# Attention and MLP on one core: token pairs side by side in the transposed tiles, the product with v in four pieces, and two moves in the MLP

## The chip, the core and the metric

The kernel runs on one core of one Trainium2 chip. The core has five engines that work side by side, each through its own list of instructions in order: TensorE (PE, with its weight loads shown apart as PEld), VectorE (DVE), ScalarE (ACT), GpSimd (POOL) and SyncE (SP), which here only issues DMAs. PE writes to the PSUM memory alone; DVE and ACT read from there; all else lies in SBUF. The metric is the device time of one execution in microseconds, lower being better.

## The reference

Eight batches of eight heads, 576 tokens, 64 elements a head. Nyström attention with 32 landmarks, then a layer norm and an MLP of 512 to 2048 to 512 with a residual:

```python
q_lm = q.reshape(B, H, m, S // m, D).mean(axis=3)      # m = 32, 18 tokens each
k_lm = k.reshape(B, H, m, S // m, D).mean(axis=3)
A  = sm(q, k_lm)            # softmax(scale * q @ k_lm^T)
Bm = sm(q_lm, k_lm)
C  = sm(q_lm, k)
Z = Bm.transpose(0, 1, 3, 2) / (norm_1(Bm) * norm_inf(Bm) + 1e-06)
for _ in range(6):
    Z = 2 * Z - Z @ Bm @ Z
x = A @ Z @ C @ v           # then heads side by side: [8, 576, 512]
xn = (x - mean) / sqrt(var + 1e-06) * g_ln
out = x + maximum(xn @ w_ch1, 0.0) @ w_ch2
```

## The kernel before

Two lines of work are woven together. The attention runs over five sets of batches, (0), (1), (2,3), (4,5), (6,7), as generators that `yield` a weight after each step. The MLP runs as one stream (`mlp`) over nine groups of 512 tokens; it yields after about every matmul. After an attention step of weight n, the main loop (L814 to L818) lets the stream take n times `rates[set]` steps. So PE's order is fixed by hand, and all matmuls are pinned in it (`MM`, `TR`: L67 and L71 in every profile). In the beginning the other engines are pinned too (`pin`, L63); from set (1) on (L794) the tile framework orders DVE, ACT and POOL itself.

A unit w is four heads of a batch. For sets (2,3) onward, `prep` (L457) makes the operands of the next set while this one runs: for k and for q of each unit, a DVE transpose in 32x32 blocks of 32-bit words (L465, two fp16 elements x of a head's 64 travel together) writes `xT`, and a DVE reduce (L469) sums the 18 tokens of each landmark into `lmk` or `lmq`. There are 8 such steps a set, 24 in all; `plans` says at which attention steps they, and the loads of q, k and v of the coming batches, are released (L806 to L810).

`attention2` (L494) then computes, in steps: the landmark softmax (`psb`); the scores of the landmarks with all keys, two units a step (`scores`, tiles `psec`), whose exponentials ACT writes to `ec` (L490) and DVE transposes into `ecT` (L528); the norm of the landmark matrix (`psse`); the product with v (`pscv`, L553 to L565), 288 matmuls of 32x32 weights on 65 columns, without a yield inside; six steps of the iteration (`psn`, with DVE's `st`, L587), the first two of which also make the scores of the queries (`psea`, `ea`); the combined matrix (`zcbd`, L605); and, in `rows_of` (L431), ten steps that give rows x of 128 tokens (`psy`, `xblk`), with the layer norm's statistics (`block_done`).

In the transposed tile, position (j, l, x) holds token 18l + j, so a fixed j gives 32 tokens that are 18 apart. ACT writes the exponentials in the order (b, l, x) with j = 2b + x, from scores that lie as (j, l).

In the MLP, POOL makes the normalised rows `xn` (for group 0, ACT does), PE transposes them into `psxt`, and DVE copies that to `xnT` (L680). Then `psh` = w1 x `xnT` in 64 matmuls on 512 columns, ACT's Relu into `hT` (L726), `pso` = `hT` x w2 in four blocks of 16 matmuls, and DVE adds the residual into `ot` (L744). Group 0 works on 128 columns at a time, since its blocks come one after the other. `psh`, `psxt` and `pso` share three PSUM buffers.

Of the kernel before, what the change touches and what calls it, by code (L numbers as in the profile page):

```python
# [20 lines left out]
def kernel(  # L21
# [58 lines left out]
    def act(*args, **kw):  # L80
        pin(nc.scalar.activation(*args, **kw))  # L81
# [375 lines left out]
    def prep(bs):  # L457
        units = [(b, u) for b in bs for u in range(U)]
        lm = {nm: asm.tile([P, len(units), LM, 2], FP16, name="lm" + nm, tag="lm" + nm)
              for nm in ("q", "k")}  # L460
        xT = {}
        for w, (b, u) in enumerate(units):
            for nm in ("k", "q"):
                t = aprep.tile([P, SEG, LM, 2], FP16, name="xT", tag="xT")
                nc.vector.transpose(  # L465
                    t[:].rearrange("p j l x -> p (j l x)").bitcast(UINT32),
                    nat_tiles[b][nm, u][:].rearrange("p j d -> p (j d)").bitcast(UINT32))
                with nc.allow_low_precision("landmark sums are rounded once, to fp16"):
                    nc.vector.tensor_reduce(out=lm[nm][:, w, :, :].rearrange("p l x -> p (l x)"),  # L469
                                            in_=t[:].rearrange("p j l x -> p (l x) j"),  # L470
                                            axis=AX.X, op=ALU.add)
                xT[nm, w] = t
                yield lm, xT

    def scores(pair, lm, xT, sc, name):
        tiles = {w: ps2.tile([P, SEG, LM], FP32, name="ps" + name, tag="p2") for w in pair}
        for (j0, j1) in ((0, 16), (16, SEG)):
            for x in range(2):
                for w in pair:
                    for h in range(4):  # L480
                        rows = ds(32 * h, 32)
                        cb = 32 * ((h + 2 * (w % 2)) % 4)
                        MM(tiles[w][ds(cb, 32), j0:j1, :], lm[rows, w, :, x],
                           xT[w][rows, j0:j1, :, x], rb=32 * h, cb=cb,
                           start=(x == 0), stop=(x == 1), skip=True)
        res = []
        for w in pair:
            t = aexp.tile([P, NJ, LM, 2], FP16, name=name, tag="e")
            act(t[:].rearrange("p b l x -> p b x l"),
                tiles[w][:].rearrange("p (b x) l -> p b x l", x=2), AF.Exp, scale=sc)  # L490
            res.append(t)
        return res

    def attention2(bs, lm, xT):  # L494
# [30 lines left out]
        for y in range(W // 2):  # L525
            for x, e in enumerate(scores((2 * y, 2 * y + 1), lm["q"], kT, sc_C, "ec")):
                t = aexp.tile([P, NJ, LM, 2], FP16, name="ecT", tag="e")
                nc.vector.transpose(t[:].rearrange("p b l x -> p (b l x)").bitcast(UINT32),  # L528
                                    e[:].rearrange("p b l x -> p (b l x)").bitcast(UINT32))
                ecT[2 * y + x] = t  # L530
            yield 4

# [45 lines left out]
        for it in range(6):  # L578
            lo = 0 if it < 5 else LM
            psn = p1([P, W, LM + D], "psn")  # L580
            for w in range(W):
                for h in range(4):
                    sl = ds(32 * h, 32)
                    MM(psn[sl, w, lo:], st[sl, w, 0:LM], st[sl, w, lo:],
                       rb=32 * h, cb=32 * h)
            stn = asm.tile([P, W, LM + D], FP16, name="st", tag="st")
            nc.vector.scalar_tensor_tensor(out=stn[:, :, lo:], in0=st[:, :, lo:], scalar=2.0,  # L587
                                           in1=psn[:, :, lo:], op0=ALU.mult,
                                           op1=ALU.subtract)
            st = stn  # L590
            if it < W // 2:
                for e in scores((2 * it, 2 * it + 1), lm["k"], qT, sc_A, "ea"):
                    ea.append(e[:].rearrange("p b l x -> p (b l x)"))
            yield 4
        pszc = ps2.tile([P, 2, 512], FP32, name="pszc", tag="p2")
        zcbd = []
# [76 lines left out]
    def transpose_block(g, u):  # L673
        if u == 0:
            xnTs[g] = mxnT.tile([P, KCH, 512], FP16, name="xnT", tag="xnT")
        xn = xn_of.pop(4 * g + u)
        psxt = psM.tile([P, KCH, P], FP16, name="psxt", tag="pm")
        for c in range(KCH):
            TR(psxt[:, c, :], xn[:, ts(c, P)], ident16[:])
        nc.vector.tensor_copy(out=xnTs[g][:, :, ts(u, P)], in_=psxt[:])  # L680

    def transposes(g):
        for u in range(4):
# [5 lines left out]
    def mlp():  # L689
        for g in range(NGRP):  # L690
            hT = mhT.tile([P, MCH, 512], FP16, name="hT", tag="hT")
            if g == 0:
                for u in range(4):
                    if u == 0:
                        transpose_block(0, 0)
                        yield True
                    for m0 in range(0, MCH, 4):
                        if m0 == 8 and u < 3:
                            transpose_block(0, u + 1)
                            yield True  # L700
                        psh = psM.tile([P, 4, P], FP32, name="psh", tag="pm")
                        for m in range(4):
                            for c in range(KCH):
                                MM(psh[:, m, :], w1_16[:, c, ts(m0 + m, P)],
                                   xnTs[0][:, c, ts(u, P)],
                                   start=(c == 0), stop=(c == KCH - 1), skip=True)
                            if m < 3:
                                yield True
                        act(hT[:, m0:m0 + 4, ts(u, P)], psh[:], AF.Relu)
                        yield True  # L710
            else:
                while g not in xnTs:
# [138 lines left out]
```

## Time and profile before

| | us |
|---|---|
| time, median of 3 runs | 381.94 (381.19 to 384.49) |
| the profiled execution's own time | 383.65 |
| its span, first to last instruction | 381.9 |

All numbers below come from the profiled execution. In its tables, "busy" is the time in which an engine had an instruction in work, "idle before" is an engine's idle time just before the instructions of a group, with what ended it, and "xN" is a count. "issue" as what ended an idle time says that the engine waited for nothing that the profile shows. The granted clock is 1.0 or, after idle stretches of PE, 0.5.

### The profile page before, as it was taken

What the parts mean: (1) busy time and instruction counts of PE and PEld (TensorE: products, weight loads), DVE (VectorE), ACT (ScalarE), POOL (GpSimd) and SP (SyncE); (2) the same over time, 40 slices, a digit from 0 to 9 for tenths busy, and PEclk for the clock granted to TensorE, in tenths of its full rate; (3) what the DMA queues carried; (4) which work ended last, traced back from release to release, by engine and by line L of the source; (5) the groups of instructions that cost most, each with busy time, mean ns of one, the idle gap of its engine ahead of it and who ended that gap; (6) DMA issues with size and microseconds to landing.
All of it is one profiled execution on the core that took longest, in us unless ns stands there. A gap on an engine that the chain in (4) does not pass through costs nothing.

```text
span 381.9 us, 8898 instructions
## 1 busy us (share of the span) xinstructions
PE 327.9 (86%) x3837; PEld 170.1 (45%) x3837; DVE 209.0 (55%) x406; ACT 130.9 (34%) x235; POOL 94.6 (25%) x147
## 2 busy tenths in 40 slices
PE   3639776594889999487999997999999999999995
PEld 3418665232434454243444544444445444444442
DVE  3473669988996796949655841146566012012011
ACT  3575633030145118131062064403602611612610
POOL 2468643047320435540030300001213002000000
PEclk9857969998699999879999999899999999999999
DMA  8999999069910129931210310022013013013013
GB/s 294 337 368 401 260 329 167 2 213 381 224 41 3 27 65 363 323 81 29 56 29 0 84 27 3 3 57 58 0 37 76 0 27 84 0 29 83 0 31 80
DMA packets 21336, 44.63 MB, mean 117 GB/s; under 512 B 2864, under 2 KB 9008, under 8 KB 21296
## 3 DMA queue, kind: packets, MB, share of 16 engines
q1 hardware_dynamic: 19184, 41.95, 36.4%
q0 software_dynamic: 2112, 2.10, 3.4%
q8 instruction: 30, 0.49, 0.6%
q14 instruction: 10, 0.08, 0.1%
HBM read 36.70 MB, written 9.44 MB: 121 GB/s over the span
## 4 chain that ended last, share of the span: by engine, by line
PE 66%; DVE 14%; DMA 8%; issue 8%; POOL 2%; SPq 0%; ACT 0%; DVEq 0%
PE psh L67 30%; PE pso L67 27%; DMA stg<-in_v_dram 5%; DMA w1stg<-in_moe_w_ch_dram 4%; DVE lmk L469 3%; DVE xT L465 3%; DVE lmq L469 3%; PE psy L67 2%; PE psxt L71 2%; PE pscv L67 2%; DVE xblk L446 1%; PE psn L67 1%; DVE st L587 1%; DVE ot L744 1%; POOL xn L652 1%
## 5 line engine op out<-in xcount | busy, mean ns | idle before, releaser
L67 PE MATMUL psh<-xnT,w 128*128 128x512 f16 (+1 forms) x768 | 140.5, 338 | 5.8 <-issue 4.7
L67 PE MATMUL pso<-w,hT 128*128 128x512 f16 x576 | 139.8, 385 | 0.0
L81 ACT ACTIVATE hT<-psh 128x512 f16<-128x512 f32 x144 | 85.1, 598 | 148.0 <-PE psh L67 147.7
L67 PEld LDWEIGHTS <-w 128*128 128x128 f16 x768 | 67.3, 103 | 65.1 <-issue 11.8
L67 PEld LDWEIGHTS <-hT 128*128 128x128 f16 x576 | 54.2, 99 | 55.9 <-issue 2.6
L744 DVE TENSOR_TENSOR ot<-pso,xblk 128x512 f32<-128x512 f32 x36 | 24.7, 685 | 68.1 <-PE pso L67 68.0
L649 POOL TENSOR_SCALAR negmr<-rstd,mvg 128x1 f32<-128x1 f32 x32 | 7.7, 261 | 145.1 <-ACT rstd L81 145.1
L652 POOL TENSOR_SCALAR xn<-xblk,rstd,negmr 128x512 f16<-128x512 f32 x32 | 24.2, 764 | 30.5 <-PE psxt L71 30.5
L136 POOL CAST nat<-stg 128x1152 f16<-128x1152 f32 x24 | 27.3, 1147 | 13.8 <-DMA stg<-in_q_dram 7.1
L446 DVE TENSOR_TENSOR xblk<-psy,rcpd 128x512 f32<-128x512 f32 (+1 forms) x40 | 27.4, 687 | 2.2 <-DMA stg<-in_v_dram 0.5
L469 DVE TENSOR_REDUCE lmq<-xT 128x64 f16<-128x1152 f16 x12 | 25.4, 2116 | 0.1
L469 DVE TENSOR_REDUCE lmk<-xT 128x64 f16<-128x1152 f16 x12 | 25.3, 2104 | 0.0
L627 DVE BATCH_NORM_STATS2 st<-xblk 128x6 f32<-128x512 f32 x36 | 24.7, 690 | 0.7
L680 DVE COPY xnT<-psxt 128x512 f16<-128x512 f16 x36 | 15.1, 419 | 17.6 <-PE psxt L71 17.4
L67 PE MATMUL psy<-zcbd,ea 128*128 128x260 f16 (+1 forms) x80 | 16.9, 293 | 6.8 <-DVE xblk L446 5.1
L67 PE MATMUL pscv<-natv,ecT 32*32 32x65 f16 x864 | 8.4, 202 | 15.3 <-issue 15.3
L445 DVE RECIPROCAL rcpd<-psy 128x8 f32<-128x8 f32 (+1 forms) x40 | 8.1, 203 | 21.8 <-PE psy L67 21.5
L465 DVE STREAM_TRANSPOSE xT<-nat 128x576 uint32<-128x576 uint32 x24 | 17.6, 758 | 2.7 <-POOL nat L136 2.1
L143 POOL CAST natv<-stg 128x1152 f16<-128x1152 f32 x12 | 13.8, 1151 | 20.1 <-DMA stg<-in_v_dram 17.0
L67 PE MATMUL psn<-st 32*32 32x96 f16 (+1 forms) x384 | 10.0, 212 | 8.8 <-DVE st L396 3.3
L71 PE MATMUL psxt<-ident,xn 128*128 128x128 f16 x144 | 14.6, 227 | 3.0 <-ACT xn L81 3.0
L81 ACT ACTIVATE ea<-psea 128x576 f16<-128x576 f32 x12 | 8.9, 810 | 24.3 <-PE psea L67 24.3
(97 smaller groups left out, 200.2 us busy)
## 6 DMA issues: line engine op xcount, KB each, us to landing
stg<-in_q_dram SPq DMA_DIRECT2D x16, 576.0 KB, 7.2
stg<-in_k_dram SPq DMA_DIRECT2D x16, 576.0 KB, 7.5
out_dram<-ot SPq DMA_DIRECT2D x72, 128.0 KB, 2.3
stg<-in_v_dram SPq DMA_DIRECT2D x10, 576.0 KB, 10.1
w1stg<-in_moe_w_ch_dram SPq DMA_DIRECT2D x16, 256.0 KB, 6.7
stg<-in_v_dram SPq DMA_DIRECT2D x12, 288.0 KB, 10.6
w<-in_moe_w_ch_dram POOLq DMA_DIRECT2D x4, 512.0 KB, 25.0
g_sb<-in_moe_g_ln_dram SPq DMA_DIRECT2D x1, 2.0 KB, 9.6
```

Source lines behind the costliest of these rows:

```text
L67: keep(nc.tensor.matmul(o, l, r, start=start, stop=stop, tile_position=(rb, cb), skip_group_check=(skip or cb != 0)))
L71: keep(nc.tensor.matmul(o, i_, idn, is_transpose=True, tile_position=(0, 0)))
L81: pin(nc.scalar.activation(*args, **kw))
L136: nc.gpsimd.tensor_copy(out=t[:], in_=stg[:])
L143: nc.gpsimd.tensor_copy(out=natv[:, ds(SEG * u, SEG), 0:D], in_=stg[:])
L446: nc.vector.tensor_tensor(out=xb[rows, :].rearrange("s (u h e) -> s u h e", u=U, e=D), in0=py[:, :, :, 0:D], in1=rcpd[rows, :, :, None].br ...
L465: nc.vector.transpose(t[:].rearrange("p j l x -> p (j l x)").bitcast(UINT32), nat_tiles[b][nm, u][:].rearrange("p j d -> p (j d)").bitcast ...
L469: nc.vector.tensor_reduce(out=lm[nm][:, w, :, :].rearrange("p l x -> p (l x)"), in_=t[:].rearrange("p j l x -> p (l x) j"), axis=AX.X, op= ...
L627: nc.vector.bn_stats(out=st6[:], in_=x_blk[j][:])
L652: nc.gpsimd.tensor_scalar(out=xn[:], in0=x_blk[4 * g + i][:], scalar1=rstd[:, k_:k_ + 1], scalar2=negmr[:, i:i + 1], op0=ALU.mult, op1=ALU ...
L680: nc.vector.tensor_copy(out=xnTs[g][:, :, ts(u, P)], in_=psxt[:])
L744: nc.vector.tensor_tensor(out=ot[:], in0=pso[:], in1=x_blk.pop(j)[:], op=ALU.add)
```

## The change

1. `xT` is laid out as (c, l, y, x), token 18l + 2c + y: the two tokens of a pair lie side by side. The transpose writes its 32 words of a block at every second word, the landmark sum runs over c and y, the scores come out in the order of the tokens' pairs, and ACT writes them without a stride.
2. The product with v yields 6 after each half of each pair of units: four pieces of 72 matmuls instead of one of 288. The rates fall from 2.0, 2.7, 2.7 to 1.8, 2.35, 2.35, and the steps of plans 2 and 3 that lie behind the product are counted three later.
3. Group 0 of the MLP works on 256 columns, two times.
4. From group 1 on, ACT instead of DVE copies `psxt` to `xnT`.

```diff
@@ prep @@
-                t = aprep.tile([P, SEG, LM, 2], FP16, name="xT", tag="xT")
+                t = aprep.tile([P, NJ, LM, 2, 2], FP16, name="xT", tag="xT")
+                words = t[:].rearrange("p c l y x -> p (c l y x)").bitcast(UINT32)
                 nc.vector.transpose(
-                    t[:].rearrange("p j l x -> p (j l x)").bitcast(UINT32),
-                    nat_tiles[b][nm, u][:].rearrange("p j d -> p (j d)").bitcast(UINT32))
+                    words.rearrange("p (c l y) -> p c y l", l=LM, y=2),
+                    nat_tiles[b][nm, u][:].rearrange("p j d -> p (j d)").bitcast(UINT32)
+                    .rearrange("p (c y l) -> p c y l", y=2, l=LM))
...
-                    nc.vector.tensor_reduce(out=lm[nm][:, w, :, :].rearrange("p l x -> p (l x)"),
-                                            in_=t[:].rearrange("p j l x -> p (l x) j"),
-                                            axis=AX.X, op=ALU.add)
+                    nc.vector.tensor_reduce(out=lm[nm][:, w, :, :],
+                                            in_=t[:].rearrange("p c l y x -> p l x c y"),
+                                            axis=AX.XY, op=ALU.add)
@@ scores @@
-        for (j0, j1) in ((0, 16), (16, SEG)):
+        for (j0, j1) in ((0, 8), (8, NJ)):
...
-                           xT[w][rows, j0:j1, :, x], rb=32 * h, cb=cb,
+                           xT[w][rows, j0:j1, :, :, x], rb=32 * h, cb=cb,
...
-            act(t[:].rearrange("p b l x -> p b x l"),
-                tiles[w][:].rearrange("p (b x) l -> p b x l", x=2), AF.Exp, scale=sc)
+            act(t[:], tiles[w][:].rearrange("p c t -> p (c t)"), AF.Exp, scale=sc)
@@ attention2, product with v @@
         for y in range(W // 2):
             for j in range(SEG):
+                if j == NJ:
+                    yield 6
...
+            if y + 1 < W // 2:
+                yield 6
@@ transpose_block @@
-        nc.vector.tensor_copy(out=xnTs[g][:, :, ts(u, P)], in_=psxt[:])
+        if g == 0:
+            nc.vector.tensor_copy(out=xnTs[g][:, :, ts(u, P)], in_=psxt[:])
+        else:
+            nc.scalar.copy(xnTs[g][:, :, ts(u, P)], psxt[:])
@@ mlp, group 0 @@
-                for u in range(4):
+                for u in (0, 2):
                     if u == 0:
-                        transpose_block(0, 0)
-                        yield True
-                    for m0 in range(0, MCH, 4):
-                        if m0 == 8 and u < 3:
-                            transpose_block(0, u + 1)
+                        for i in range(2):
+                            transpose_block(0, i)
                             yield True
-                        psh = psM.tile([P, 4, P], FP32, name="psh", tag="pm")
-                        for m in range(4):
+                    for m0 in range(0, MCH, 2):
+                        if u == 0 and m0 in (6, 10):
+                            transpose_block(0, 2 if m0 == 6 else 3)
+                            yield True
+                        psh = psM.tile([P, 2, 256], FP32, name="psh", tag="pm")
+                        for m in range(2):
                             for c in range(KCH):
                                 MM(psh[:, m, :], w1_16[:, c, ts(m0 + m, P)],
-                                   xnTs[0][:, c, ts(u, P)],
+                                   xnTs[0][:, c, ds(P * u, 256)],
...
-    rates = [0, 1.0, 2.0, 2.7, 2.7]
+    rates = [0, 1.0, 1.8, 2.35, 2.35]
-    plans = {1: (-1, 2, -1, 7, range(9, 17)), 2: (0, 2, 5, 5, range(7, 15)),
-             3: (0, 2, 5, 5, range(7, 15))}
+    plans = {1: (-1, 2, -1, 7, range(9, 17)), 2: (0, 2, 8, 8, range(10, 18)),
+             3: (0, 2, 8, 8, range(10, 18))}
```

PE's order in the product with v of batches 4 and 5. Before, the last matmuls of the first pair of units (`natv0` holds v of batch 4, `ecT` the transposed exponentials) are followed at once by those of the second pair:

```order
L67 MATMUL pscv_2920<-natv0_104,ecT_2788 32x65
L67 LDWEIGHTS ecT_2844
L67 MATMUL pscv_2920<-natv1_106,ecT_2844 32x65
L67 LDWEIGHTS ecT_2844
L67 MATMUL pscv_2920<-natv1_106,ecT_2844 32x65
```

The same product after the change, at the end of its first piece:

```order
L67 LDWEIGHTS ecT_2678
L67 MATMUL pscv_2804<-natv0_104,ecT_2678 32x65
L67 LDWEIGHTS w1_16_132
L67 MATMUL psh_2800<-xnT_2391,w1_16_132 128x512
L67 LDWEIGHTS hT_2479
L67 MATMUL pso_2879<-w2_16_133,hT_2479 128x512
```

One matmul of `psh` and 13 of `pso` now stand between the first and the second piece, where the product's own next matmul stood.

ACT's order in set (2,3), from the exponentials of the key scores (`ec`) to the statistics of the next rows (`lnv`). Before:

```order
L81 ACTIVATE ec<-psec 128x9x2x32 x4
L81 ACTIVATE ea<-psea 128x9x2x32 x4
L81 ACTIVATE hT<-psh 128x512 x16
L81 ACTIVATE lnv<-mvg,eps_ln 128x4
L81 ACTIVATE rstd<-lnv 128x4
```

After:

```order
L81 ACTIVATE ec<-psec 128x576 x4
L688 COPY xnT<-psxt 128x4x128 x4
L81 ACTIVATE hT<-psh 128x512 x4
L81 ACTIVATE ea<-psea 128x576 x2
L81 ACTIVATE hT<-psh 128x512 x2
L81 ACTIVATE ea<-psea 128x576 x2
L81 ACTIVATE hT<-psh 128x512 x10
```

The four copies to `xnT` have come onto ACT, and four of the Relus of the next MLP group have moved ahead of the query exponentials `ea`, since the product's pieces now let the MLP run on.

DVE's order in the same set, from the end of the product (`rcv`, the row sums' reciprocal) into the iteration (`st`). Before:

```order
L569 RECIPROCAL rcv_2031<-pscv_1742 128x4
L570 TENSOR_TENSOR rcv_2031<-rcv_2031,cinv_1720 128x4
L571 TENSOR_TENSOR st_1722<-pscv_1742,rcv_2031 128x4x64
L680 COPY xnT_1671<-psxt_2038 128x4x128
L587 SCALAR_TENSOR_TENSOR st_2065<-st_1722,psn_2048 128x384
L465 STREAM_TRANSPOSE xT_2376<-nat_1690 128x576
L465 STREAM_TRANSPOSE xT_2405<-nat_1686 128x576
L680 COPY xnT_1671<-psxt_2109 128x4x128
L469 TENSOR_REDUCE lmk_2237<-xT_2376 128x64
L587 SCALAR_TENSOR_TENSOR st_2149<-st_2065,psn_2132 128x384
```

After:

```order
L574 RECIPROCAL rcv_1953<-pscv_1606 128x4
L575 TENSOR_TENSOR rcv_1953<-rcv_1953,cinv_1589 128x4
L576 TENSOR_TENSOR st_1591<-pscv_1606,rcv_1953 128x4x64
L592 SCALAR_TENSOR_TENSOR st_1984<-st_1591,psn_1967 128x384
L466 STREAM_TRANSPOSE xT_2281<-nat_1559 128x9x2x32
L466 STREAM_TRANSPOSE xT_2303<-nat_1555 128x9x2x32
L471 TENSOR_REDUCE lmk_2149<-xT_2281 128x64
L592 SCALAR_TENSOR_TENSOR st_2066<-st_1984,psn_2049 128x384
```

The two copies to `xnT` are gone from this part; the transposes and the sum still stand between two steps of the iteration.

More of the change, by code (lines that the diff above doesn't have):

```diff
@@ L475, in scores @@
     def scores(pair, lm, xT, sc, name):
-        tiles = {w: ps2.tile([P, SEG, LM], FP32, name="ps" + name, tag="p2") for w in pair}
-        for (j0, j1) in ((0, 16), (16, SEG)):
+        tiles = {w: ps2.tile([P, NJ, 2 * LM], FP32, name="ps" + name, tag="p2") for w in pair}
+        for (j0, j1) in ((0, 8), (8, NJ)):
             for x in range(2):
@@ L692, in mlp @@
             if g == 0:
[L693 removed]
+                for u in (0, 2):
                     if u == 0:
[L695 to L702 removed]
+                        for i in range(2):
+                            transpose_block(0, i)
+                            yield True
+                    for m0 in range(0, MCH, 2):
[4 more added lines that the diff above has]
+                        for m in range(2):
                             for c in range(KCH):
                                 MM(psh[:, m, :], w1_16[:, c, ts(m0 + m, P)],
[L705 removed]
+                                   xnTs[0][:, c, ds(P * u, 256)],
                                    start=(c == 0), stop=(c == KCH - 1), skip=True)
[L707 to L709 removed]
+                                if c == 1 or (c == 3 and m == 0):
+                                    yield True
+                        act(hT[:, m0:m0 + 2, ds(P * u, 256)], psh[:], AF.Relu)
                         yield True
```

6 lines of the change are left out of this document (3 added, 3 removed).

## The prediction

> **What bounds the kernel now.** I read the page's engine shares and slices first, then the chain that ended last.
>
> ```profile
> span 381.9 us, 8898 instructions
> PE 327.9 (86%) x3837; PEld 170.1 (45%) x3837; DVE 209.0 (55%) x406; ACT 130.9 (34%) x235; POOL 94.6 (25%) x147
> PE   3639776594889999487999997999999999999995
> DVE  3473669988996796949655841146566012012011
> PE 66%; DVE 14%; DMA 8%; issue 8%; POOL 2%; SPq 0%; ACT 0%; DVEq 0%
> ```
>
> The chain is PE's, except in two kinds of place: where DVE is full (slices 5 to 12) and where "issue" stands, PE waiting for nothing that the profile shows. I therefore cut the run into four stretches. A (44.9 to 80.5) is the attention of batch 1 after its product with v; B (80.5 to 116.9) and C (146.5 to 188.5) are batches 2, 3 and 4, 5 up to the last step of the iteration; D (230 to 245) surrounds the product of batches 6, 7. A window's columns are its length, busy time of PE, PEld, DVE, ACT and POOL, the clock granted, DMA share and GB/s.
>
> ```profile
> 44.90:80.50 35.60, 23.17 (x297) 14.49 (x289) 32.14 (x49) 6.93 (x12) 9.19 (x8) 0.86 0.65 155
> 80.50:116.90 36.40, 27.25 (x613) 13.71 (x614) 32.47 (x47) 10.77 (x18) 17.56 (x20) 0.86 0.71 221
> 146.50:188.50 42.00, 32.99 (x667) 16.28 (x666) 31.62 (x40) 11.86 (x19) 13.78 (x12) 0.92 0.55 174
> 230.00:245.00 15.00, 12.40 (x386) 6.57 (x385) 2.72 (x9) 5.51 (x10) 0.00 (x0) 0.89 0.02 3
> ```
>
> In A, DVE is busy 32.1 of 35.6 us: it is the bound. In B, PE idles 9.15 us and DVE 3.9. In C and D PE is the engine, idle for 9.0 and 2.6 us. Outside these stretches and the loading at the start PE is nearly full, so the change can win there only in them.
>
> The "issue" idle stands inside the products with v:
>
> ```profile
> 44.90 0.23 PE L67 MATMUL psh<-xnT,w 128*128 128x128 f16 x1
> 49.80 0.48 PE L67 MATMUL psh<-xnT,w 128*128 128x128 f16 x3 [4.67 <-issue]
> ...
> 90.03 1.26 PE L67 MATMUL pscv<-natv,ecT 32*32 32x65 f16 x128 [1.36 <-issue]
> 96.23 0.56 PE L67 MATMUL pscv<-natv,ecT 32*32 32x65 f16 x43 [4.93 <-issue]
> ...
> 155.39 1.82 PE L67 MATMUL pscv<-natv,ecT 32*32 32x65 f16 x194
> 163.65 0.99 PE L67 MATMUL pscv<-natv,ecT 32*32 32x65 f16 x94 [6.43 <-issue]
> ...
> 233.51 1.88 PE L67 MATMUL pscv<-natv,ecT 32*32 32x65 f16 x208
> 237.99 0.81 PE L67 MATMUL pscv<-natv,ecT 32*32 32x65 f16 x80 [2.60 <-issue]
> ...
> q8 instruction: 30, 0.49, 0.6%
> ```
>
> Between the two stops of the first of these products lie 128 matmuls, and with the weight load of each 256 instructions. The instruction queue (packets, MB, share) moved 30 packets, and PE ran 2 x 3837 instructions: 256 a packet. So I read each stop as PE reaching the end of a block before the next block is there. From block to block it took 90.03 to 96.23, 6.2 us. In the next product the block before began 66 matmuls in, at about 155.39 + 66/194 x 1.82 = 156.0, and the stop ended at 163.65: 7.6 us. In D the same reckoning, 80 matmuls in, gives 234.2 to 237.99, 3.8 us; there the DMA share is 0.02. A block of the product is used up in 1.3 us.
>
> After such a stop the clock is halved for a while:
>
> ```profile
> 47.60:54.30 6.70, 4.50 (x55) 3.50 (x54) 3.71 (x5) 1.68 (x3) 3.35 (x4) 0.50 1.08 327
> 92.00:102.10 10.10, 5.58 (x103) 3.03 (x103) 9.34 (x11) 0.00 (x0) 5.39 (x5) 0.50 0.99 286
> 160.20:166.90 6.70, 3.25 (x100) 1.72 (x100) 3.02 (x6) 0.60 (x1) 2.30 (x2) 0.50 0.77 181
> 238.70:242.00 3.30, 3.30 (x20) 1.19 (x9) 0.77 (x3) 0.60 (x1) 0.00 (x0) 0.50 0.02 5
> ```
>
> Half of the PE time in these four windows is what the clock cost: 2.2, 2.8, 1.6 and 1.6 us.
>
> **The change part by part.** The prices come from these groups and the last pieces of one MLP group:
>
> ```profile
> L469 DVE TENSOR_REDUCE lmk<-xT 128x64 f16<-128x1152 f16 x12 | 25.3, 2104 | 0.0
> L512 DVE TENSOR_REDUCE rsum<-psb 128x4 f32<-128x128 f32 x3 | 0.8, 280 | 2.1 <-ACT psb L81 2.1
> L324 DVE TENSOR_REDUCE rsum<-psb 128x2 f32<-128x64 f32 x2 | 0.4, 222 | 0.2 <-ACT psb L81 0.2
> L465 DVE STREAM_TRANSPOSE xT<-nat 128x576 uint32<-128x576 uint32 x24 | 17.6, 758 | 2.7 <-POOL nat L136 2.1 <-PE psea L67 0.5
> L528 DVE STREAM_TRANSPOSE ecT<-ec 128x288 uint32<-128x288 uint32 x12 | 5.6, 475 | 6.3 <-ACT ec L81 6.2
> L81 ACT ACTIVATE ec<-psec 128x576 f16<-128x576 f32 x12 | 8.9, 808 | 2.7 <-PE psec L67 2.6
> L81 ACT ACTIVATE ect<-psc 128x576 f16<-128x576 f32 x4 | 2.4, 648 | 0.4 <-PE psc L67 0.4
> L680 DVE COPY xnT<-psxt 128x512 f16<-128x512 f16 x36 | 15.1, 419 | 17.6 <-PE psxt L71 17.4
> L81 ACT ACTIVATE hT<-psh 128x512 f16<-128x512 f32 x144 | 85.1, 598 | 148.0 <-PE psh L67 147.7
> 306.40 7.77 PE pso L67 x36
> ...
> 320.28 0.42 DVE L680 COPY xnT<-psxt 128x512 f16<-128x512 f16 x1 [1.52 <-PE psxt L71]
> 320.94 0.38 PE L67 MATMUL psh<-xnT,w 128*128 128x512 f16 x1
> ```
>
> The landmark sums, 24 of them. Before, each element read lies 128 bytes from the last, and 1152 elements take 2104 ns. The reduces of a dense row cost (280 - 222)/64 = 0.9 ns an element, which makes 1.21 us of 1152; DVE's transposes cost (758 - 475)/288 = 0.98 ns an element, 1.32 us with their fixed part. After, elements come as neighbours 4 bytes apart and then a jump. I take 1.35 us, near the dense rows, and keep 1.21 and 2.10 as ends: 0.75 us less each, 6.0 for the eight in a stretch.
> [...]
>
> The 24 transposes write every second word instead of every word. 758 ns is kept; the dearest bound is the old reduce's 1.83 ns an element, 1.2 us.
>
> Scores read the same 512 columns with the same 4-byte step, so PE's price stays. The 24 exponentials write densely, 648 ns for 808; ACT sits idle most of the time, 34% busy on the page, so 0.
>
> The product in four steps. The step weights grow by 3 x 6 = 18. Until the iteration's end B releases 65 x 1.8 = 117 MLP steps instead of 47 x 2.0 = 94, 23 more; C (from the first scores) 62 x 2.35 instead of 44 x 2.7, 27 more. A step is a matmul of 7.77/36 = 0.216 us, so 5.0 and 5.8 us of work that is taken out of later time. Between pieces of 72 product matmuls (0.7 us) now lie about 11 MLP matmuls in B and 14 in C and D, so 128 matmuls take some 4.6 us in B and 5.5 in C and D. Against 3.8 nothing is left to wait in D; against 6.2, 1.6 us a block in B, and against 7.6, 2.1 in C. With two or three blocks each, and those lengths measured at full DMA load, I take about half: 2.4 in B, 2.2 in C. Ends are 0 and the old stops.
>
> Loads of v and the preparation steps move to three numbers later, which is the same place behind the product: six issues on SP, four casts on POOL, needed by the next product tens of us later. Cost 0.
>
> The 32 copies of transposed LN rows leave DVE (1.6 us less in B and in C). On ACT one costs about 0.59 by the hT row. At a group's end the DVE copy ends at 320.70 and the next psh starts at 320.94, so 0.17 more is covered; where exponentials stand ahead of it on ACT it isn't. I take 0.7 for all, ends 0 and 3.
>
> The first group on 256 columns streams the same columns with half the weight loads, but needs block 1 before its first matmul: between -1 and +1, taken as 0, since A behind it is DVE's. It also shifts the ends of blocks: by the order, one falls at the start of batch 1's product and the next some 7 us of work later. The 4.67 stop shrinks to about 1.
>
> Sum. A: DVE 32.1 - 6.0 - 0.4 (a copy that comes earlier) = 25.7, plus 1.9 of waits left = 27.6, gain 8.0; PE's 23.2 fits under it. B: PE 27.25 - 2.8 + 5.0 + 2.4 + 0.7 of other waits = 32.5, over DVE's 24.9; gain 36.4 + 5.0 - 32.5 = 8.9. C: 33.0 - 1.6 + 5.8 + 2.2 = 39.4; gain 42.0 + 5.8 - 39.4 = 8.4. D: 2.6 + 1.6 = 4.2. Less 0.7: 28.8 us. The profiled execution took 383.65 us, 1.7 above the median of 381.94 and within the spread of the runs. 383.65 - 28.8 = 354.9, so 355.
>
> **The rivals.** The landmark sums stay at 2.10 us. For it: no row shows a reduce in this pattern, and half of the steps still jump. Then A gains 2.7 (DVE 31.7 + 1.2), B 8.1 (DVE 30.8 + 2.5 of waits is just its bound), C 7.9, D 4.2, less 0.7: 22 us, 361.
>
> The stops stay whole. For it: the wait is then not a matter of how fast a block is used up. Against it: the first block end inside the second and third of these products passed without a stop. With 20 us of idle and the clock loss kept, A gains 5.0, B 2.8, C 2.6, D 0, less 0.7: 10 us, 374.
> [...]
>
> Slower: DVE's patterns cost by the run. The exponential with 18 strided rows takes 160 ns more than the dense one, 8.9 ns a row; the new reduce has 576 runs of two. At half of that a reduce would cost 2.6 us more than my 1.35, 1.84 more than now; the sixteen in A and B are on the path (29 us), the eight in C over about 9 us of slack (6 us): 35 against the 22 of the first rival, 396. It decides from 1.2 us more a preparation, about 2 ns a run. Against it: DVE's other strided rows show nothing like it.
>
> **How the numbers follow.** Forecast (355, own range 347 to 361): 0.66. Sums stay at 2.10 (361): 0.16. Stops stay whole (374): 0.10. Slower (396): 0.04. Gains lost elsewhere, such as ACT's copies holding PE, near 381: 0.04. About 1%, 3.8 us, can be told from no change; so faster by over 1% has 0.92, within 1% 0.04, slower 0.04. Low is 355 less the page waits left (4.6) and the reduces at 1.21 (1.1) and the 1.7 of the profiled execution, about 347; high takes in the first rival with the stops half kept, 369. That leaves out the other cases and a rest of the first two, 0.2.
>
> **What would show it.** Right: reduces of 1.2 to 1.5 us, transposes near 0.76; products in pieces of 72 with "issue" under 5 us in all, none in D; clock 1.0 from 140 on; xnT copies on ACT near 0.59 with psh starting at once; A near 28 us with DVE still full. Wrong: reduces of 2.1 or more, stops of 4 us or more between pieces, psn waiting for DVE in B, or psh waiting for ACT at the starts of groups.

## The result, and the profile after

| | before | after |
|---|---|---|
| time, median | 381.94 us (382.0 with a fourth run) | 356.3 us (355.05 to 356.87) |
| the profiled execution's own time | 383.65 us | 355.05 us |
| its span | 381.9 us | 353.4 us |

The ratio of the times is 0.9313, with a 95% interval of 0.9264 to 0.9362: about 26 us faster. In a second series (11 runs of the kernel before, 6 after) it was 0.9282 (0.9255 to 0.9309).

The engine shares, two engines' slices, the granted clock and the chain, from the page of the kernel after:

```profile
span 353.4 us, 8636 instructions
...
PE 320.7 (91%) x3709; PEld 163.0 (46%) x3709; DVE 178.3 (50%) x374; ACT 145.9 (41%) x267; POOL 94.6 (27%) x147
...
PE   3745979698989899999999999999999999999994
...
DVE  2654699969668689458466641234765010020011
...
PEclk9955999999999999999999999999999999999999
...
PE 72%; DVE 14%; DMA 7%; issue 3%; POOL 2%; SPq 0%; ACT 0%
```

"issue" has gone from 8% of the chain to 3%, and from 34.6 us on the clock is whole until 352.0, 1.4 us before the end. TensorE works 7.2 us less and is idle 21.3 us less (span less busy time: 32.7 for 54.0).

Where the time was won needs a fair cut, since the new rates release more MLP work by a given step. I take the same steps of the attention in both kernels and count the MLP steps that stand ahead of them in PE's order, at 0.216 us each. The windows are those between these steps, with the columns of the prediction's windows; batch 1's attention from its product on, batches 2, 3, batches 4, 5, and batches 6, 7, each from its first landmark matmul (`psb`) to its combined matrix (`pszc`). Before:

```profile
44.20:77.90 33.70, 21.76 (x324) 14.28 (x327) 30.08 (x45) 6.89 (x12) 9.19 (x8) 0.85 0.69 163
77.90:118.00 40.10, 30.46 (x660) 14.92 (x659) 35.07 (x53) 11.86 (x20) 17.56 (x20) 0.87 0.66 205
...
144.30:188.30 44.00, 34.99 (x690) 17.16 (x689) 32.70 (x44) 13.37 (x23) 13.78 (x12) 0.92 0.56 179
...
222.60:260.20 37.60, 35.00 (x696) 17.23 (x695) 11.15 (x27) 13.62 (x23) 0.00 (x0) 0.95 0.12 27
```

After:

```profile
45.10:68.30 23.20, 18.36 (x248) 10.93 (x247) 22.86 (x41) 6.99 (x12) 9.20 (x8) 1.00 0.89 223
68.30:105.80 37.50, 33.29 (x691) 15.96 (x693) 28.36 (x51) 16.06 (x30) 17.59 (x20) 1.00 0.70 219
...
131.60:172.20 40.60, 39.83 (x717) 19.11 (x716) 25.04 (x42) 17.90 (x32) 14.20 (x13) 1.00 0.58 176
...
202.60:242.20 39.60, 39.60 (x723) 19.21 (x722) 10.57 (x25) 18.13 (x33) 0.00 (x0) 1.00 0.13 29
```

| stretch | shorter by | MLP steps more | won | forecast |
|---|---|---|---|---|
| start, to batch 1's product | -0.9 | -1 | -1.1 | 0 |
| A: to `psb` of batches 2, 3 | 10.5 | 1 | 10.7 | 8.0 |
| B: to `pszc` of batches 2, 3 | 2.6 | 23 | 7.6 | 8.9 |
| to `psb` of batches 4, 5 | 0.5 | -10 | -1.7 | |
| C: to `pszc` of batches 4, 5 | 3.4 | 27 | 9.2 | 8.4 |
| to `psb` of batches 6, 7 | 3.9 | -18 | 0.0 | |
| D: to `pszc` of batches 6, 7 | -2.0 | 27 | 3.8 | 4.2 |
| the rest | 10.5 | -49 | -0.1 | -0.7 |

The sum is 28.4 of the span's 28.5 us. A and B are best read together (18.3 won, 16.9 forecast), since the prediction cut between them 2.6 us later, at the first scores. In A VectorE is still full (22.86 of 23.20); in C and D TensorE now is.

The groups that the prediction priced, after:

```profile
L471 DVE TENSOR_REDUCE lmk<-xT 128x64 f16<-128x1152 f16 x12 | 15.9, 1322 | 0.0
L466 DVE STREAM_TRANSPOSE xT<-nat 128x576 uint32<-128x576 uint32 x24 | 17.7, 757 | 3.0 <-POOL nat L136 2.1
L688 ACT COPY xnT<-psxt 128x512 f16<-128x512 f16 x32 | 18.7, 586 | 85.0 <-PE psxt L71 85.0
L81 ACT ACTIVATE ec<-psec 128x576 f16<-128x576 f32 x12 | 7.1, 648 | 2.9 <-PE psec L67 2.9
```

And the product of batches 2, 3 on TensorE's timeline (start, length, instructions, idle time ahead of them):

```profile
78.08 0.75 PE L67 MATMUL pscv<-natv,ecT 32*32 32x65 f16 x72
...
81.03 0.44 PE L67 MATMUL pscv<-natv,ecT 32*32 32x65 f16 x35
82.09 0.45 PE L67 MATMUL pscv<-natv,ecT 32*32 32x65 f16 x37 [0.62 <-issue]
...
85.80 0.75 PE L67 MATMUL pscv<-natv,ecT 32*32 32x65 f16 x72
...
89.29 0.75 PE L67 MATMUL pscv<-natv,ecT 32*32 32x65 f16 x72
```

0.62 us is all that is left of the stops of 1.36 and 4.93 us; in the other two products none is left.

### The profile page after: what moved, and what is told of

Same layout as the page of the kernel before. It is cut to its first block, busy times and chain, and to the rows that moved or that the text cites. A ratio compares the mean times of both kernels' runs of the same rounds, so it can differ in the third digit from the quotient of the medians.

```text
span 353.4 us, 8636 instructions
## 1 busy us (share of the span) xinstructions
PE 320.7 (91%) x3709; PEld 163.0 (46%) x3709; DVE 178.3 (50%) x374; ACT 145.9 (41%) x267; POOL 94.6 (27%) x147
## 4 chain that ended last, share of the span: by engine, by line
PE 72%; DVE 14%; DMA 7%; issue 3%; POOL 2%; SPq 0%; ACT 0%
PE psh L67 31%; PE pso L67 30%; DMA stg<-in_k_dram 5%; DVE xT L466 3%; DVE lmk L471 2%; PE psy L67 2%; DMA stg<-in_q_dram 2%; PE psn L67 2%; PE psxt L71 2%; PE pscv L67 2%; DVE xblk L446 2%; DVE lmq L471 2%; DVE st L632 1%; DVE ot L753 1%; PE pst L71 1%
## 5 line engine op out<-in xcount | busy, mean ns | idle before, releaser
L67 PE MATMUL pso<-w,hT 128*128 128x512 f16 x576 | 137.8, 379 | 2.1 <-DMA w<-in_moe_w_ch_dram 2.1
L67 PE MATMUL psh<-xnT,w 128*128 128x512 f16 (+1 forms) x640 | 137.0, 361 | 1.4 <-DVE ot L753 0.9
L67 PEld LDWEIGHTS <-w 128*128 128x128 f16 x640 | 60.1, 99 | 58.2 <-issue 3.1
L67 PEld LDWEIGHTS <-hT 128*128 128x128 f16 x576 | 53.3, 98 | 56.4 <-issue 3.9
L688 ACT COPY xnT<-psxt 128x512 f16<-128x512 f16 x32 | 18.7, 586 | 85.0 <-PE psxt L71 85.0
L71 PEld LDWEIGHTS <-xn 128*128 128x128 f16 x144 | 11.1, 100 | 14.9 <-ACT xn L81 4.7
L592 DVE SCALAR_TENSOR_TENSOR st<-st,psn 128x384 f16<-128x384 f16 (+1 forms) x18 | 9.5, 527 | 15.8 <-PE psn L67 15.8
L471 DVE TENSOR_REDUCE lmq<-xT 128x64 f16<-128x1152 f16 x12 | 16.1, 1344 | 0.1
L471 DVE TENSOR_REDUCE lmk<-xT 128x64 f16<-128x1152 f16 x12 | 15.9, 1322 | 0.0
```

The costliest lines, as they stand in the source:

```text
L67: keep(nc.tensor.matmul(o, l, r, start=start, stop=stop, tile_position=(rb, cb), skip_group_check=(skip or cb != 0)))
L71: keep(nc.tensor.matmul(o, i_, idn, is_transpose=True, tile_position=(0, 0)))
L471: nc.vector.tensor_reduce(out=lm[nm][:, w, :, :], in_=t[:].rearrange("p c l y x -> p l x c y"), axis=AX.XY, op=ALU.add)
L688: nc.scalar.copy(xnTs[g][:, :, ts(u, P)], psxt[:])
```

## The experiments

Each was compared with runs of the kernel before on the same chip; 1% is 3.8 us. The changed kernel itself was measured only in the series of the last four, so elsewhere a difference from it goes across series, and its own two ratios, 0.9313 and 0.9282, lie 1.2 us apart. Times at a step of the attention are comparable directly where PE's order is that of the changed kernel.

**The product's pieces without work between them.**

```diff
                 if j == NJ:
-                    yield 6
+                    yield 0
...
             if y + 1 < W // 2:
-                yield 6
+                yield 0
...
                     ea.append(e)
-            yield 4
+            yield 7
```

> The changed kernel, but the three yields inside the product with v release nothing; the 18 weights go to the six steps of the iteration (7 instead of 4 each), so as many MLP steps are released by the iteration's end and rates and plans stay. Theory of the pace (a block of 256 PE instructions must not be used up faster than the next one comes): the product's 288 matmuls run at 1.3 us a block again, so 'issue' idle returns inside the products, 5 to 6 us in the first, 6 to 7 in the second, about 2.5 in the third, and after them the halved clock, together 15 to 20 us: 371 to 376 us. Rival (the gain comes from more MLP steps ahead of the iteration's end, wherever they stand): within 2 us of the changed kernel's 356.3.

Measured: 365.5 us, ratio 0.9562 (0.9529 to 0.9595). TensorE's timeline in the three products, and two windows:

```profile
81.91 1.29 PE L67 MATMUL pscv<-natv,ecT 32*32 32x65 f16 x128 [2.22 <-issue]
87.84 0.54 PE L67 MATMUL pscv<-natv,ecT 32*32 32x65 f16 x40 [4.63 <-issue]
...
151.30 0.99 PE L67 MATMUL pscv<-natv,ecT 32*32 32x65 f16 x102 [2.01 <-issue]
...
223.33 0.95 PE L67 MATMUL pscv<-natv,ecT 32*32 32x65 f16 x97 [2.12 <-issue]
```

```profile
82.00:88.00 6.00, 1.37 (x155) 1.23 (x160) 5.20 (x6) 0.00 (x0) 3.96 (x4) 0.52 0.63 254
...
149.30:151.30 2.00, 0.00 (x0) 0.00 (x0) 1.26 (x3) 0.00 (x0) 0.19 (x1) 1.00 0.00 0
```

The stops are back, with as many MLP steps released as in the changed kernel, so the rival falls: it is the pace at which the product uses up its instructions. Only their size was below the expectation (371 to 376 us). The stop in the product of batches 4, 5 was 2.0 us instead of 6.4, and here no transfer was under way (DMA share 0.00), where it was 1.04 before. The reason is on SyncE's list: in the kernel before, the six loads of v for batches 6, 7 were issued from 151.3 us on, ahead of the product (155.4); here stores of the MLP's results stand ahead of them, and they came at 160.1, behind the product (147.5). In the changed kernel they are behind it too (157.7 against 141.4). So some 2 of the 6.4 us are the pace alone; the rest went with these loads, as the experiment on them below bears out (2.2 us). Of the 9.3 us by which the profiled span is longer, 0.5 stood already at the start of the first product (2.1 at `psb`, behind a wait of 3.0 us for w2); 5.7 arose in B from there on, 0.9 in C and 2.3 in D.

**The old layout in the changed kernel** (the hunks of `prep`, `scores` and the exponentials turned back).

> The changed kernel with xT, the landmark sums, the scores and the exponentials as before. Theory: the eight sums of batch 1's attention stand on the path, since VectorE is busy there 22.9 of 23.1 us, so 8 x 0.77 = 6.2 us come back there; in the stretch of batches 2, 3 VectorE rises to 33.4 us of 35, so up to 3 more; behind that TensorE is the bound and nothing is lost: 362 to 366 us, VectorE full between 46 and 75 us, no more 'issue' than in the changed kernel. Rival (the stretch got shorter because its stop and its halved clock went): within 2 us of 356.3.

Measured: 373.8 us, ratio 0.9765 (0.9719 to 0.9811): 17 us lost, where 6 to 10 were expected. Windows of A and B, and B's waits of TensorE:

```profile
44.80:74.80 30.00, 20.90 (x248) 11.83 (x247) 28.36 (x40) 7.07 (x12) 9.21 (x8) 0.89 0.71 176
74.80:121.80 47.00, 38.69 (x683) 17.45 (x682) 35.39 (x52) 17.03 (x30) 17.60 (x20) 0.85 0.55 175
```

```profile
PE psn L67 <- DVE st L591: 3.9, 1, 3.9
PE psxt L71 <- DVE ot L752: 2.4, 1, 2.4
PE psec L67 <- DVE xblk L446: 1.5, 2, 0.9
```

A is 6.8 us longer, as expected. B is 9.5 us longer although VectorE is busy only 35.4 of its 47 us, and C, where nothing should have been lost, 4.0 us (44.6 for 40.6). In B TensorE waits for VectorE for 8 us, and the clock is 0.85 on the mean of these 47 us: TensorE's busy time is 5.4 us more for the same work. My expectation took the larger of two engines' busy times as a stretch's length; here the engines waited for each other in turn.

**The same sums in another order of reading.**

```diff
-                                            in_=t[:].rearrange("p c l y x -> p l x c y"),
+                                            in_=t[:].rearrange("p c l y x -> p l x y c"),
```

> The changed kernel, but the landmark sum reads its tile with c inside and y outside: the same data, the same layout, the same sums, but each element now lies 256 bytes from the last instead of every second one 4 bytes away. Theory (a read far from the last one costs, a neighbour comes free): the sum takes 2.0 to 2.2 us again, VectorE fills batch 1's attention and the stretch of batches 2, 3 as with the old layout, 368 to 375 us. Rival (the price is the count of elements and of dimensions): 1.3 to 1.4 us and 355 to 358 us.

Measured: 373.0 us, ratio 0.9733 (0.9699 to 0.9767). The group of the sums:

```profile
L471 DVE TENSOR_REDUCE lmk<-xT 128x64 f16<-128x1152 f16 x12 | 25.3, 2105 | 0.0
```

Nothing but the distance between successive reads changed, and the sum takes 2105 ns again instead of 1322: at 128 bytes from one element to the next it took 2104 ns, at 256 bytes 2105, and with a neighbour behind each jump it takes 0.78 us less. So part 1 wins by its pairs alone, and its whole worth hangs on them.

**Copies of the LN rows on VectorE.**

```diff
-        if g == 0:
-            nc.vector.tensor_copy(out=xnTs[g][:, :, ts(u, P)], in_=psxt[:])
-        else:
-            nc.scalar.copy(xnTs[g][:, :, ts(u, P)], psxt[:])
+        nc.vector.tensor_copy(out=xnTs[g][:, :, ts(u, P)], in_=psxt[:])
```

> The changed kernel with all copies of transposed LN rows on VectorE, as before. Theory: they are hidden on either engine, 32 x 0.42 us on a VectorE that is half idle from 104 us on and has no such copy in batch 1's attention: 355.5 to 357.5 us. Rival (they delay the iteration's st on VectorE in batches 2 to 7): psn waits for st once or twice in each set, 358 to 361 us.

Measured: 360.6 us, ratio 0.943 (0.9393 to 0.9466), 4 to 5 us slower than the changed kernel. VectorE's timeline in the product of batches 2, 3:

```profile
84.33 1.42 DVE L466 STREAM_TRANSPOSE xT<-nat 128x576 uint32<-128x576 uint32 x2
85.68 1.31 DVE L471 TENSOR_REDUCE lmk<-xT 128x64 f16<-128x1152 f16 x1
86.91 1.34 DVE L471 TENSOR_REDUCE lmq<-xT 128x64 f16<-128x1152 f16 x1
88.17 0.41 DVE L685 COPY xnT<-psxt 128x512 f16<-128x512 f16 x1
```

The last copy stands behind two transposes and two sums; `psh`, which the split now lets run between the pieces, waited 2.73 us for it, and the clock was halved for 3.4 us after it. The time lies in the rival's range, but not by its mechanism: `psn` waits 1.6 us for `st` in B, as in the changed kernel, and it is `psh` that is late. Of the 4.9 us by which the profiled span is longer, 2.6 arose in B from the start of the product on. Another 1.9 stood at that start (2.9 at `psb`), ahead of any copy that the edit touches, with a wait of 3.3 us for w2 and a halved clock. Why that came out longer in this kernel is open, so 2.6 us is what the trace lets be put down to these copies.

**Group 0 on 128 columns** (its hunk turned back).

> The changed kernel with group 0 of the MLP on 128 columns, as before. It has 128 matmuls more, 256 PE instructions, so the ends of blocks behind group 0 stand where they stood. Theory: the stop of some 4.7 us in batch 1's attention returns with its halved clock; VectorE, which is the bound there, waits 3.3 us for it as before, and the start is about 1 us earlier: 357.5 to 360 us. Rival (the stop went because the landmark sums no longer hold TensorE's work together, not through group 0): no stop over 1 us between 44 and 60 us, 355 to 357 us.

Measured: 358.7 us, ratio 0.9389 (0.9361 to 0.9418), 2 to 4 us slower. The stop is back, right behind batch 1's product:

```profile
48.91 1.76 PE L67 MATMUL psh<-xnT,w 128*128 128x128 f16 x15 [4.02 <-issue]
```

By PE's order, laid beside the trace, the block that ends there (256 instructions) began at 42.09 us. TensorE had used it up by 44.89, and the next one came at 48.91: 6.8 us from block to block. This block ends one matmul behind the product, which fills most of it. In the changed kernel 60 matmuls of `psh` fewer stand ahead of the product (56 for 116), so a block ends at the product's start and the next one, from 45.28 to 52.03, holds the rest of the product and 24 matmuls of `psh` on 256 columns, each twice as long as one on 128 (109 ns from one to the next, for 56 in the kernel before). TensorE took 6.76 us for it, 1.96 of them a wait for VectorE's `st`, and the next block was there. What of this is the place of the block's end and what the longer instructions, these two kernels don't separate.

**The layout alone, on the kernel before** (the hunks of part 1).

> The kernel before with the new layout of xT alone (part 1). Theory (the parts cover each other: undone one by one from the changed kernel they cost 17, 9, 4 and 2 us, 32 together, for 26 won): the stops in the products and the halved clock after them stay, so the layout alone wins 6 in batch 1's attention and 3 to 8 behind it, 368 to 373 us, with 15 us of 'issue' in the products. Rival (the layout's gain does not depend on the others): the 17 us that its undoing cost, 364 to 367 us.

Measured: 375.7 us, ratio 0.9831 (0.9766 to 0.9895), above the expected range: 6.5 us won. "issue" idle behind 38 us was 20.5 us (21.2 in the kernel before): 14.0 inside the products, 4.8 in group 0, 1.7 at `psn`.

**The split alone, on the kernel before** (the yields, rates and plans of part 2).

> The kernel before with the product in four steps, the new rates and plans alone (part 2). Theory: 'issue' idle inside the products falls from 15 to under 2 us, but with the old sums VectorE holds TensorE in batch 1's attention and in batches 2, 3, and the gaps so made halve the clock; what is won is the stops of the last two products (6.4 and 2.6 us) with their halved clock (3 us), less than the 9 us that undoing the split cost where it had VectorE's help only if the second stretch loses too: 372 to 378 us. Rival (nothing is won while VectorE is the bound): 380 to 384 us.

Measured: 379.1 us, ratio 0.9899 (0.986 to 0.9937), some 4 us won, between the theory's range and the rival's. TensorE's timeline in B:

```profile
99.94 0.59 PE L67 MATMUL psh<-xnT,w 128*128 128x512 f16 x1 [4.72 <-DVE xnT L684]
...
119.22 0.51 PE L67 MATMUL psn<-st 32*32 32x96 f16 x16 [3.85 <-DVE st L591]
```

No stop is left in the products, but `psh` waits 8.0 us in all for VectorE's copies. One part gives 6.5 and the other 4 us alone; undoing the layout costs 17, pressing the product's pieces together 9. The new rates and plans were not run without the split. The split lets the MLP run between the pieces only where VectorE hands it its rows in time, which the new layout and ACT's copies bring about.

**The loads behind the product, on the kernel before.**

```diff
-    plans = {1: (-1, 2, -1, 7, range(9, 17)), 2: (0, 2, 5, 5, range(7, 15)),
-             3: (0, 2, 5, 5, range(7, 15))}
+    plans = {1: (-1, 2, -1, 7, range(9, 17)), 2: (4, 5, 7, 8, range(9, 17)),
+             3: (4, 5, 7, 8, range(9, 17))}
```

> The kernel before with the loads of q and k of the next batches, and the preparation steps, moved behind the product with v (plans 2 and 3 only). The product is not split. Theory (a block of PE instructions comes later when the data loads hold the DMA engines: 6 to 7.6 us with them, 3.3 to 3.8 without): the stop in the product of batches 4, 5 shrinks from 6.4 to 2 to 2.6 us, and that of batches 2, 3 from 4.9 to under 3.5, with a shorter halved clock: 372 to 379 us. Rival (a block takes its time whatever the data loads do): stops of 6 and 5 us as before, 381 to 385 us.

Measured: 379.3 us, ratio 0.9898 (0.986 to 0.9937), just above the expected range. The stops in the three products:

```profile
92.16 0.50 PE L67 MATMUL pscv<-natv,ecT 32*32 32x65 f16 x43 [2.34 <-issue]
...
159.99 0.93 PE L67 MATMUL pscv<-natv,ecT 32*32 32x65 f16 x94 [2.19 <-issue]
234.19 0.81 PE L67 MATMUL pscv<-natv,ecT 32*32 32x65 f16 x80 [2.01 <-issue]
```

6.43 and 4.93 us have become 2.19 and 2.34, near the third (2.01), which never had loads beside it. So these loads had lengthened the time from block to block. The time gained is small, some 4 us: the preparation now stands between the product and the iteration, where `psh` waits 3.8 us for VectorE's copies (0.5 before) and `psn` 4.2 us for `st` (3.2 before).

**The changed kernel again, and two tries to better it.** In both tries all loads of w2 are issued ahead of the casts of batch 1's v. In the second, also:

```diff
+                    s = t
+                    if bs[0] == 2:
+                        s = aprep.tile([P, 5, LM, 2, 2], FP16, name="xs", tag="xs", bufs=2)
+                        nc.gpsimd.tensor_tensor(out=s[:, 0:4], in0=t[:, 0:4], in1=t[:, 4:8],
+                                                op=ALU.add)
+                        nc.gpsimd.tensor_copy(out=s[:, 4:5], in_=t[:, 8:9])
```

> The changed kernel once more, word for word, as the measure for the next two. 355 to 357 us. Theory: in its profile no halved clock between 35 and 350 us, unless TensorE waits over about 2 us for the w2 weights in batch 1's attention, as in two of the kernels above.

> The changed kernel with all four loads of w2 issued ahead of the casts of batch 1's v, so the last two 2.3 us earlier. Theory (TensorE's waits for w2, 2.1 us in the changed kernel and 3.2 and 3.3 in two others, with a halved clock there, hold VectorE's work in batch 1's attention too): these waits fall under 0.5 us, 353 to 355 us. Rival (VectorE is full there in any case, 22.9 of 23.1 us): within 0.7 us of the changed kernel.

> As the kernel with the early loads of w2, and GpSimd adds c 0 to 3 and 4 to 7 of each tile of batches 2 and 3 ahead of VectorE's landmark sum, which then reads 640 elements instead of 1152. Theory (VectorE alone bounds batch 1's attention, 22.9 of 23.1 us; GpSimd is busy 9 of 23 there): a sum takes about 0.8 us instead of 1.33, 4 us less on VectorE, 350 to 353 us. Rival (GpSimd's adds come late or slow VectorE down, and VectorE waits for them): 355 to 360 us.

Measured: 355.5, 355.9 and 356.0 us; ratios 0.9282 (0.9255 to 0.9309), 0.9299 (0.9267 to 0.9331), 0.9299 (0.9274 to 0.9324). Neither try wins. The first kernel's profile has a halved stretch at 49.7 to 53.2 us that the expectation didn't have: it follows a wait of 1.93 us for VectorE's `st`, not one for w2. The early issue left the wait for w2 at 2.6 us, so it isn't the issue that is late. With GpSimd's adds a sum of 640 elements took 0.81 us and VectorE's load in A fell to 19.2 of 24 us, but GpSimd rose to 19.8 and VectorE waited 2.8 us for it.

**Pauses put into TensorE's work.** In the changed kernel, after the 4th and 15th `psh` of the last three groups:

```diff
+                    if (g, m) in GAP:
+                        t0 = mout.tile([P, 4], FP16, name="gs", tag="gs")
+                        nc.vector.tensor_copy(out=t0[:, 0:2], in_=xnT[:, 0, 0:2])
+                        ta = xpool.tile([P, DM], FP32, name="ga", tag="ga", bufs=2)
+                        nc.vector.tensor_copy(out=ta[:], in_=psh[:])
+                        for _ in range(GAP[g, m]):
...
+                        nc.vector.scalar_tensor_tensor(out=xnT[:, 0, 0:2], in0=ta[:, 0:2],
+                                                       scalar=0.0, in1=t0[:, 0:2],
+                                                       op0=ALU.mult, op1=ALU.add)
```

> The changed kernel with six pauses of TensorE put into the last three MLP groups, where nothing else waits: after the 4th and the 15th psh of a group VectorE copies psh, works N times more on 512 columns, and then writes back two columns of xnT unchanged, for which the next matmul waits. N is 0, 1, 2, 3, 4, 6; by the rows of VectorE on 512 columns the pauses should be about 0.9, 1.5, 2.1, 2.7, 3.3 and 4.5 us. Theory (a pause of over about 2 us is followed by a halved clock, which costs 1.7 or 3.4 us more; a shorter one costs itself): full clock after the first two, halved after the last three for 3.4 or 6.8 us each, 376 to 384 us. Rival (the halved clock had another cause, such as the mixture of small matmuls): full clock throughout, 370 to 373 us.

Measured: 382.5 us (one run). The last four pauses on TensorE's timeline, and three windows:

```profile
304.40 9.67 PE L67 MATMUL psh<-xnT,w 128*128 128x512 f16 x44 [2.60 <-DVE xnT L748]
317.13 1.89 PE L67 MATMUL psh<-xnT,w 128*128 128x512 f16 x4 [3.06 <-DVE xnT L748]
341.22 12.63 PE L67 MATMUL psh<-xnT,w 128*128 128x512 f16 x44 [3.52 <-DVE xnT L748]
358.30 1.89 PE L67 MATMUL psh<-xnT,w 128*128 128x512 f16 x4 [4.45 <-DVE xnT L748]
```

```profile
316.50:319.90 3.40, 2.77 (x7) 1.04 (x8) 0.47 (x2) 0.60 (x1) 0.00 (x0) 0.50 0.00 0
...
340.40:347.20 6.80, 5.98 (x15) 2.13 (x16) 0.79 (x4) 1.79 (x3) 0.00 (x0) 0.50 0.00 0
...
357.50:364.30 6.80, 6.00 (x15) 2.15 (x16) 0.60 (x3) 0.60 (x1) 0.00 (x0) 0.50 0.01 2
```

The pauses of 2.36, 2.14 and 2.60 us left the clock whole; those of 3.06, 3.52 and 4.45 halved it for 3.4, 6.8 and 6.8 us. The first two pauses came out longer than the 0.9 and 1.5 us worked out ahead, so none under 2 us was tried, and the three that left the clock whole are all over the 2 us of the theory: length alone doesn't decide (see the last section). Six pauses of 18.1 us in all made the span 25.9 us longer than in the changed kernel's second profile (380.8 against 354.9). The rest, 7.8 us, is the halved clock: half of TensorE's busy time in the three windows is 7.4 us. So here it followed from the pause, not from the kind of matmul.

## Why the prediction was right

**The sum.** 28.8 us were forecast and 28.5 measured, on the span. The mechanisms of the sum, dearer landmark sums and stops at block ends, are borne out below; that the number came so close is partly luck. The stretches were up to 3 us off each way: A won 2.7 more, B 1.3 less, and the start and the passage to batches 4, 5, for which I had taken nothing, lost 2.8. Errors of 4.1 us one way and 4.5 the other cancelled.

**The landmark sums.** 1.35 us taken, 1.32 and 1.34 measured, and the experiment on their reading order shows that the pairs are the cause. A sum took 2105 ns where each element read lies 256 bytes from the last, and 1322 where every second one is a neighbour.

**The transposes** write at every second word for the same price, 757 ns for 758; the exponentials take 648, as taken.

**The stops.** Mechanism right, size off: I left 1, 2.4 and 2.2 us in A, B and C, and 0, 0.6 and 0 remained. With the MLP between the pieces TensorE took 4.2 to 7.2 us to use up a block in C and D, and no block came later than that; I had reckoned with 5.5 us of use against 7.6 of waiting. The 7.6 us didn't return in C, since the loads of v, which I took to stand behind the product in both kernels, come behind it only now: the DMA share there is 0.08 and 0.24 in the first two blocks, where it was 1.04 before, and beside few or no transfers the next block came after 3.3 to 3.9 us elsewhere. So in C part 2 acted by two ways, the pieces and the later loads, and I had named one. Of the signs named as wrong one showed a little: `psn` waited 1.6 us for VectorE's `st` in B.

**A.** 27.6 us were forecast from behind the product to the main run of the first scores (44.9 to 80.5 before); the changed kernel took 25.5 for it (45.97 to 71.49). By the common cut, up to `psb`, 10.7 us were won, not 8.0. I kept 1 us of the stop, 1.9 of waits and VectorE's row work that now falls behind `psb` instead of ahead of it (VectorE has 41 instructions there, not 45).

**LN copies on ACT.** This step failed in its sign. I took a cost of 0.7 us; moving them won 4 to 5 by the undoing, at least 2.6 of it by the trace. I compared two lengths, 0.42 and 0.59 us, and left out that on VectorE the copy queues behind the preparation (`psh` waited 2.73 us for it in B), while the split makes `psh` need it sooner.

**Group 0 on 256 columns.** Its own price was taken as 0, and A's stop was to shrink to 1 us because the ends of blocks shift. They did: an end fell at the product's start and the next 6.76 us later, as forecast, and no stop was left. (Only behind group 0 do the ends stand as before, since 128 matmuls less are exactly one block.) Taking this part away costs 2 to 4 us, more than the 0 that it was given.

**The rivals.** "Sums stay at 2.10" was priced at 361; the kernel that has just this took 373. The step that failed is the price of B, where I let the longer of two engines set the time: gained 8.1, which makes some 37 us from `psb` to `pszc`, and that kernel took 46.0. In its place the runs showed pauses of TensorE behind VectorE's queue and the halved clock after them (in B of the kernel with the old layout waits of 8 us and a clock of 0.85). "Stops stay whole" fell: the kernel with the pieces pressed together has them again. No run shows a price by the run of two elements: 576 of them cost less, not more.

## What to carry to other kernels

Parts of a change that feed one another can't be priced one by one: here two parts gave 6.5 and 4 us alone, while in the whole undoing the one cost 17 and pressing the other's pieces together 9. When two streams are woven on one engine, ask of each stretch not only which engine is fuller but which handover stands behind what on the other engine, and add what the halved clock costs behind long pauses (7.8 us behind three of the six pauses above). And the products' 288 matmuls on 65 columns ran out of instructions here, with stops of up to 6.4 us: with larger matmuls between their pieces 0.6 us of stops was left, and with the loads moved behind them the stops of 6.4 and 4.9 us were 2.2 and 2.3.

## What the runs showed of the hardware

**The halved clock followed a fixed grid.** Its stretches lasted 3.41 us or a multiple, and began at times that lie multiples of 3.41 us apart: in the kernel before at 47.54, 74.84, 91.91, 160.18 and 238.68 us, for 6.83, 3.41, 10.24, 6.83 and 3.41 us. I cut the 14 profiles from 38 us on, up to 9 us before their ends, along this grid and took TensorE's busy share in each piece at full clock: of 33 pieces under 0.42 all were followed by a halved one; of 15 between 0.42 and 0.53, six; of 1186 above that, none. In the halved pieces the same mark held if work at half clock counts half: of 60, the 21 in which TensorE was busy under 0.82 were followed by another halved one, the 39 busier ones by the whole clock. That is why a halved stretch could go on after the pause was over (6.8 us behind the pause of 3.52 above). So a pause of 2.60 us that straddled two pieces cost no clock (above), and one of 2.02 us that lay in one, at 225.9 us in the kernel with the layout alone, halved it: the 11 matmuls of `psh` behind it took 4.24 us, 11 ahead of it 2.54, so 1.7 us more. The changed kernel is close to that edge. Its pause of 1.96 us at 47.0 left the clock whole, and in its second profile one of 1.93 us at 47.3 halved it. Gaps of 1.93 and 2.02 us were enough where they lay in one piece (busy for 0.44 and 0.41 of it).

**Instruction blocks.** Counted through the 14 traces, the first matmul behind each of the 24 stops of over 0.5 us put down to "issue" (from 38 us on) has 93 matmuls and a multiple of 128 ahead of it: all stand one or more whole blocks apart. From block to block, where such a stop lay between, it took 3.3 to 3.9 us at a DMA share of 0.15 or less (six times), and 3.9 to 9.2 us at 0.64 or more (18 times). The longest stop, 6.4 us, stood inside a product of matmuls on 65 columns (batches 4, 5 in the kernel before).

**Reads of VectorE.** With pairs, a sum of 1152 elements took 1.33 us on the mean of `lmk` and `lmq`, 1.15 ns an element, against 1.83 with every element alone (2.10 us). A sum of 640 took 0.81, so 512 elements more cost 1.0 ns each.

Open: why the wait for w2 in A differed from 1.4 to 3.3 us between kernels with the same work up to there. The loads themselves took longer where it was long: 25.1 and 25.6 us from issue to landing with the waits of 3.3 and 3.2, and 23.5 to 24.4 with the others.
